# Expert layers with 64-column weight blocks on alternating column halves, tokens moving

## The chip, the cores and the metric

The kernel runs on one core of a Trainium2 chip. A core has a matrix engine (TensorE; PE for its matmuls and PEld for its weight loads in the trace), a vector engine (DVE), a scalar engine (ACT), GpSimd (POOL) and a queue engine (SP), which work beside each other and wait for each other by semaphores. Matmul results land in PSUM, eight banks of 512 fp32 values for each of 128 partitions; DVE and ACT read them there. A matmul has a stationary operand (`lhsT`, loaded into the array) and a moving one (`rhs`). The metric is device time of the whole kernel in microseconds, lower is better.

## What is computed

A recurrent attention block (rwkv7) makes 3072 tokens of 320 values each. Each token then goes to one of eight experts, at most 80 tokens for one expert:

```python
# x: (3072, 320), w1: (8, 320, 1024), w2: (8, 1024, 320), capacity 80
expert_idx = np.argmax(x @ w_gate, axis=1)
...
for e in range(E):
    tok_idx = np.where(expert_idx == e)[0]
    if len(tok_idx) > capacity:
        keep = np.argpartition(-gate_w[tok_idx], capacity)[:capacity]
        tok_idx = tok_idx[keep]
    h = np.maximum(x[tok_idx] @ w1[e], 0.0)
    out[tok_idx] = gate_w[tok_idx, None] * (h @ w2[e])
```

Everything is fp32.

## The kernel before

The attention stage takes most of the time. Its instructions are put in order by a planner in the kernel (class Plan); the change does not touch it. It works with 64x64 blocks on the four quarters of the matrix array, and it serves here as a place where small blocks can be seen: line 344 turns full 128x128 blocks (transposes by a matmul with the identity), and lines 437, 622, 655, 702 and 724 are each 16 matmuls on the four quarters.

Then the tokens of each expert are chosen (lines 1008 to 1051), which ends with the row numbers idx_g (to gather) and idx_s (to scatter). Meanwhile SP issues the weights of all experts, 2 x 320 x 1024 x 4 bytes = 2.6 MB for each, in four transfers: w1 (256 of the 320 input rows, line 978), w1r (the last 64 input rows; the first 512 hidden columns on partitions 0 to 63, the others on 64 to 127; line 980, two transfers) and w2 (line 981). Each expert has buffers of its own for them.

The expert stage is ordinary code on a tile framework, which sets the order of instructions and the semaphores by itself. For an expert e:

- gather (line 1063): POOL issues an indirect transfer of 80 token rows. All eight are issued first.
- turn_x (1067 to 1077): the rows are turned so that the 320 inputs lie on partitions (three transposes; the last 64 inputs twice, on both partition halves). DVE copies the result to xe.
- first_layer (1079 to 1091): xe is stationary (80 columns) and the weights move, 512 columns in each of four matmuls with all 128 rows (line 1085) and two with 64 rows, on the two row halves (line 1088). ACT applies relu into h, tokens on partitions.
- turn_h (1093 to 1101): eight transposes bring the 1024 hidden values onto partitions; DVE copies them to hT.
- second_layer (1103 to 1113): hT is stationary and w2 moves, eight matmuls of 320 columns into yp, tokens on partitions. DVE multiplies with the gate weight (line 1110) and POOL scatters the rows to the output (line 1111).

The main loop overlaps experts: the first layer of expert e, the turn of x for e+1, the second layer of e-1, the turn of h for e. An fp32 matmul stands in the trace as two records of TensorE (two passes), a transpose as one.

Of the kernel before, what the change touches and what calls it, by code (L numbers as in the profile page):

```python
# [8 lines left out]
F32 = mybir.dt.float32  # L9
# [3 lines left out]
Act = mybir.ActivationFunctionType  # L13
# [132 lines left out]
def kernel(  # L146
# [19 lines left out]
    nc = tc.nc  # L166
    B, H, S, D = r.shape
    N, DM = out.shape
    E = moe_w_gate.shape[1]
    F = moe_w1.shape[2]  # L170
# [885 lines left out]
    ps_h = ctx.enter_context(tc.tile_pool(name="ps_h", bufs=2, space=PSUM))  # L1056
    ps_t = ctx.enter_context(tc.tile_pool(name="ps_t", bufs=1, space=PSUM))
    ps_y = ctx.enter_context(tc.tile_pool(name="ps_y", bufs=1, space=PSUM))
    rows, xes, hs, hts = {}, {}, {}, {}

    def gather(e):
        rows[e] = fs.tile([cap, XW], F32, name="rows", tag="rows", bufs=8)
# [4 lines left out]
    def turn_x(e):  # L1067
        re = rows[e]
        tail = fs.tile([cap, 128], F32, name="twice", tag="twice")
        for i in range(2):  # L1070
            nc.scalar.copy(tail[:, 64 * i : 64 * i + 64], re[:, KW:DM])
        xp = ps_x.tile([128, 3, cap], F32, name="xp", tag="x")
        for i in range(2):
            nc.tensor.transpose(xp[:, i, :], re[:, 128 * i : 128 * i + 128], ident[:cap, :cap])
        nc.tensor.transpose(xp[:, 2, :], tail, ident[:cap, :cap])  # L1075
        xes[e] = fs.tile([128, 3, cap], F32, name="xe", tag="xe")
        nc.vector.tensor_copy(xes[e], xp)  # L1077

    def first_layer(e):
        w1, w1r, _ = weights[e]  # L1080
        xe = xes.pop(e)
        hp = [ps_h.tile([cap, FH], F32, name="hp", tag=f"h{j}") for j in range(2)]
        for i in range(2):
            for j in range(2):
                nc.tensor.matmul(hp[j], lhsT=xe[:, i, :], rhs=w1[:, i, FH * j : FH * j + FH], start=i == 0, stop=False)  # L1085
        for j in range(2):
            half = slice(64 * j, 64 * j + 64)
            nc.tensor.matmul(hp[j], lhsT=xe[half, 2, :], rhs=w1r[half, :], start=False, stop=True)  # L1088
        hs[e] = fs.tile([cap, F], F32, name="h", tag="h")
        for j in range(2):  # L1090
            nc.scalar.activation(hs[e][:, FH * j : FH * j + FH], hp[j], Act.Relu)  # L1091

    def turn_h(e):
        h = hs.pop(e)
        hts[e] = fs.tile([128, FK, cap], F32, name="hT", tag="hT")
        for j in range(2):
            tp = ps_t.tile([128, FK // 2, cap], F32, name="tp", tag=f"t{j}")
            for f in range(FK // 2):
                o = FH * j + 128 * f
                nc.tensor.transpose(tp[:, f, :], h[:, o : o + 128], ident[:cap, :cap])  # L1100
            nc.vector.tensor_copy(hts[e][:, FK // 2 * j : FK // 2 * (j + 1), :], tp)  # L1101

    def second_layer(e):
        w2 = weights[e][2]
        hT = hts.pop(e)
        yp = ps_y.tile([cap, DM], F32, name="yp", tag="y")
        for f in range(FK):
            nc.tensor.matmul(yp, lhsT=hT[:, f, :], rhs=w2[:, f, :], start=f == 0, stop=f == FK - 1)  # L1108
        y = fs.tile([cap, DM], F32, name="y", tag="y")
        nc.vector.tensor_scalar_mul(y, yp, rows[e][:, DM : DM + 1])  # L1110
        nc.gpsimd.indirect_dma_start(  # L1111
            out=out[:, :], out_offset=bass.IndirectOffsetOnAxis(ap=idx_s[:, e : e + 1], axis=0),
            in_=y[:, :], element_offset=0, bounds_check=N - 1, oob_is_err=False, in_offset=None)
# [4 lines left out]
    for e in range(E + 1):  # L1118
        if e < E:
            first_layer(e)  # L1120
        if e + 1 < E:
            turn_x(e + 1)
        if e > 0:
            second_layer(e - 1)
        if e < E:
            turn_h(e)


# [24 lines left out]
```

## Time and profile before

| what | value |
|---|---|
| median of 3 runs | 560.91 us (559.71 to 563.14) |
| the profiled execution's own time | 561.64 us |
| its span, first to last instruction | 559.6 us |
| TensorE busy with matmuls | 425.6 us, 76% of the span |
| DVE, ACT, POOL busy | 312.5, 186.0, 224.1 us |
| mean granted TensorE clock | 0.891 of 2.4 GHz |
| bytes moved by DMA | 72.91 MB, mean 130 GB/s |

The sums cover the whole span; the change concerns its last sixth alone, so they have to be read from that stretch. The slices of the page divide the span into 40 parts of 14 us, with the busy share of an engine in tenths; the timeline gives single groups of instructions in order of time, with start, length (from the first start to the last end) and count.

### The profile page before, as it was taken

Reading aid. Unit: us, or ns where it says so; the run is one execution under the profiler, and the core shown is the slowest. Engines: PE = TensorE matmul, PEld = TensorE weight load, DVE = VectorE, ACT = ScalarE, POOL = GpSimd, SP = SyncE. Lnnn points to the kernel's source line nnn. Section 1 sums busy time; section 2 is a strip of 40 time slices with the busy share of each in tenths; the row PEclk is TensorE's granted clock in tenths of the full one; section 3 lists DMA queues with packets and bytes.
Section 4 is the critical chain, followed back from the end, with each engine's and each line's share of the span. In section 5 each row is a group of like instructions: output and inputs, shape, how many; then the busy total and the mean of one; then the engine's idle time right before and its main releaser. Section 6 shows DMA issues by size and latency. Waiting matters only on the chain. (4 is left out here: it accounts for less than half of the span.)

```text
span 559.6 us, 22079 instructions
## 1 busy us (share of the span) xinstructions
PE 425.6 (76%) x9617; PEld 331.6 (59%) x9617; DVE 312.5 (56%) x706; ACT 186.0 (33%) x361; POOL 224.1 (40%) x393
## 2 busy tenths in 40 slices
PE   2644089797928988889799998998895003999996
PEld 2543078686717877778687887887784002344443
DVE  4867977444703855684476644966678981121211
ACT  2432064353512453444443643445231000101010
POOL 7010011788388410898699516981000005010101
PEclk9978569798976999999899999999699555899999
DMA  8775367556593477676577374327200049999300
GB/s 133 113 116 112 64 154 133 99 94 133 96 243 81 99 174 134 149 132 117 133 143 172 100 132 116 75 44 161 71 16 27 23 143 342 326 332 344 104 15 16
DMA packets 241444, 72.91 MB, mean 130 GB/s; under 512 B 217908, under 2 KB 235716, under 8 KB 241348
## 3 DMA queue, kind: packets, MB, share of 16 engines
q1 hardware_dynamic: 211428, 65.50, 51.6%
q10 hardware_dynamic: 29152, 4.36, 4.9%
q0 software_dynamic: 768, 1.64, 1.0%
q8 instruction: 76, 1.25, 0.9%
q14 instruction: 20, 0.16, 0.1%
HBM read 53.26 MB, written 18.13 MB: 128 GB/s over the span
## 5 line engine op out<-in xcount | busy, mean ns | idle before, releaser
L498 POOL TENSOR_TENSOR tmp<-lt 128x30 f32<-128x30 f32 (+9 forms) x150 | 84.0, 560 | 61.0 <-DMA lt<-blocks 50.3
L500 POOL TENSOR_TENSOR lt<-lt,tmp 128x30 f32<-128x30 f32 (+9 forms) x150 | 88.8, 592 | 11.8
L707 DVE TENSOR_TENSOR UL<-ps,mask 128x832 f32<-128x832 f32 x24 | 24.5, 1022 | 54.0 <-PE ps L702 54.0
L758 PE MATMUL ps<-wsel,xT 128*128 128x192 f32 x192 | 40.7, 360 | 2.3 <-DVE xT L748 1.4
L1111 POOL DMA_INDIRECT out_dram<-y,idx_s x8 | 7.3, 917 | 74.6 <-DVE y L1110 74.6
L758 PEld LDWEIGHTS ps<-wsel,xT 128*128 128x128 f32 x192 | 34.2, 208 | 4.3 <-DVE xT L748 1.7
L369 DVE TENSOR_TENSOR_SCAN P<-dec,begins 128x520 f32<-128x520 f32 x24 | 31.4, 1313 | 9.4 <-ACT dec L365 9.3
L1108 PE MATMUL yp<-w,hT 128*80 128x320 f32 x128 | 35.9, 434 | 0.5 <-DVE hT L1101 0.5
L344 PE MATMUL ps<-ident,raww 128*128 128x128 f32 x88 | 16.6, 320 | 25.5 <-DMA raww<-in_w_dram 24.4
L344 PE MATMUL ps<-ident,kb 128*128 128x128 f32 x192 | 32.8, 297 | 3.6 <-DVE ends L373 1.8
L735 DVE TENSOR_TENSOR st<-ps,st 128x832 f32<-128x832 f32 (+1 forms) x24 | 23.8, 990 | 17.9 <-PE ps L724 17.9
L485 POOL MEMSET nt<- 32x1024 f32 x12 | 11.3, 945 | 54.6 <-ACT nt L417 54.2
L377 DVE TENSOR_TENSOR_SCAN iv<-dec,ends 128x520 f32<-128x520 f32 x24 | 30.2, 1259 | 4.0 <-ACT ivc L396 3.3
L1085 PE MATMUL hp<-w,xe 128*80 128x512 f32 x64 | 31.6, 641 | 0.5 <-DVE xe L1077 0.5
L452 DVE TENSOR_TENSOR psi<-ps,mask 128x512 f32<-128x512 f32 x24 | 16.4, 686 | 27.3 <-PE ps L437 23.0
L1091 ACT ACTIVATE h<-hp 80x512 f32<-80x512 f32 x16 | 8.6, 587 | 61.5 <-PE hp L1088 61.5
L611 ACT COPY rv<-ps 128x1024 f32<-128x1024 f32 x24 | 24.3, 1014 | 11.4 <-PE ps L344 6.5
L344 PEld LDWEIGHTS ps<-ident,raww 128*128 128x128 f32 x88 | 11.5, 162 | 27.4 <-DMA raww<-in_w_dram 15.1
L1108 PEld LDWEIGHTS yp<-w,hT 128*80 128x80 f32 x128 | 18.6, 150 | 14.7 <-issue 0.8
L344 PEld LDWEIGHTS ps<-ident,kb 128*128 128x128 f32 x192 | 22.8, 149 | 7.4 <-issue 3.7
L407 DVE TENSOR_TENSOR kb<-rawkb,ps 128x640 f32<-128x640 f32 x22 | 17.9, 813 | 15.5 <-PE ps L344 13.4
L1077 DVE COPY xe<-xp 128x240 f32<-128x240 f32 x8 | 3.3, 407 | 40.9 <-PE xp L1075 40.9
(171 smaller groups left out, 961.3 us busy)
## 6 DMA issues: line engine op xcount, KB each, us to landing
w<-in_moe_w_dram SPq DMA_DIRECT2D x8, 1280.0 KB
w<-in_moe_w_dram SPq DMA_DIRECT2D x8, 1024.0 KB, 16.4
VL<-in_v_dram SPq DMA_DIRECT2D x96, 40.0 KB, 2.3
out_dram<-zero SPq DMA_DIRECT2D x8, 480.0 KB, 4.2
raww<-in_w_dram SPq DMA_DIRECT2D x44, 80.0 KB, 2.8
rawkb<-in_k_dram SPq DMA_DIRECT2D x44, 80.0 KB, 3.6
rawkb<-in_b_dram SPq DMA_DIRECT2D x44, 80.0 KB, 3.2
rawr<-in_r_dram ACTq DMA_DIRECT2D x84, 40.0 KB, 2.9
```

Of the source, the lines that this page charges most:

```text
L344: nc.tensor.matmul(o, lhsT=i, rhs=ident, start=True, stop=True, is_transpose=True, skip_group_check=True)
L369: nc.vector.tensor_tensor_scan(at("P", n), at("dec", n)[:, 0 : H * SEG], begins, 0.0, op0=Alu.mult, op1=Alu.add)
L377: nc.vector.tensor_tensor_scan(at("iv", n)[:, H * SEG : 0 : -1], at("dec", n)[:, H * SEG : 0 : -1], at("ends", n)[:, H * SEG : 0 : -1], 0. ...
L407: nc.vector.tensor_tensor(out=view(at("kb", n), 0, (HB * H, 2), (HB, H), (1, D)), in0=view(at("rawkb", n), 0, (DM, 2), (D, H), (1, D)), in ...
L498: e.tensor_tensor(out=tv, in0=t3[:, 0:s, s : s + 1].to_broadcast([128, s, n]), in1=t3[:, s : s + 1, s + 1 :].to_broadcast([128, s, n]), op ...
L500: e.tensor_tensor(out=t3[:, 0:s, s + 1 :], in0=t3[:, 0:s, s + 1 :], in1=tv, op=Alu.add)
L611: nc.scalar.copy(at("rv", n).rearrange("p (k c) -> p k c", k=2), ps[:, bank(kr) : bank(kr) + 2, :])
L707: nc.vector.tensor_tensor(out=view(at("UL", n), 0, (M4 * X, 2), (1, M4 * X)), in0=view(ps[:, bank(ku), :], 0, (512, 2), (1, M4 * X)), in1= ...
L735: nc.vector.tensor_tensor(out=view(st, o, (BS, M4), (step, 2), (1, n_)), in0=view(flat, 512 * bank(ky) + o, (4 * T, M4), (step, 2), (1, n_ ...
L758: nc.tensor.matmul(ps[:, b0, WS * m : WS * m + WX], lhsT=at("xT", n)[:, 2 * T * cof(m, 0) : 2 * T * cof(m, 0) + 2 * T], rhs=wsel_[:, WS * ...
L1085: nc.tensor.matmul(hp[j], lhsT=xe[:, i, :], rhs=w1[:, i, FH * j : FH * j + FH], start=i == 0, stop=False)
L1108: nc.tensor.matmul(yp, lhsT=hT[:, f, :], rhs=w2[:, f, :], start=f == 0, stop=f == FK - 1)
```

## The change

The expert layers swap their operands. In the first layer the weights are stationary, in blocks of 64 columns, and the 80 turned tokens move. Block b goes to column half 64 x (b mod 2) of the array, so that neighbours lie on different halves; the result has the hidden values on partitions, as the second layer needs them, and h is not turned any more. The 64 last input rows become 16 small matmuls on the four quarters. Relu is split: ACT takes the first half of the hidden values, DVE the second, both straight into hT.

In the second layer w2 is stationary in blocks of 64 of the 320 outputs, five for each of eight chunks of the hidden values, again on alternating column halves; the fifth block takes the one or the other half by turns, so that it is summed in two places. The result yp has the outputs on partitions and is copied to yT by DVE; turn_y turns it back with two transposes and one matmul against `pair`, two stacked 64x64 identities, which also adds the two halves of the fifth block. Then DVE scales as before and POOL scatters. `pair` is written by two copies on POOL. PSUM buffers: two of yp instead of one; one yq in place of two tp.

```diff
--- before.py
+++ after.py
@@ -1056,7 +1056,10 @@
     ps_h = ctx.enter_context(tc.tile_pool(name="ps_h", bufs=2, space=PSUM))
     ps_t = ctx.enter_context(tc.tile_pool(name="ps_t", bufs=1, space=PSUM))
     ps_y = ctx.enter_context(tc.tile_pool(name="ps_y", bufs=1, space=PSUM))
-    rows, xes, hs, hts = {}, {}, {}, {}
+    rows, xes, hts, yts = {}, {}, {}, {}
+    pair = fs.tile([128, HB], F32, name="pair", tag="pair", bufs=1)
+    nc.gpsimd.tensor_copy(pair[0:HB], ident[0:HB, 0:HB])
+    nc.gpsimd.tensor_copy(pair[HB:], ident[HB:, HB:])
 
     def gather(e):
         rows[e] = fs.tile([cap, XW], F32, name="rows", tag="rows", bufs=8)
@@ -1076,38 +1079,48 @@
         xes[e] = fs.tile([128, 3, cap], F32, name="xe", tag="xe")
         nc.vector.tensor_copy(xes[e], xp)
 
+    QF, NB = FK // 2, FH // 64
+
     def first_layer(e):
         w1, w1r, _ = weights[e]
         xe = xes.pop(e)
-        hp = [ps_h.tile([cap, FH], F32, name="hp", tag=f"h{j}") for j in range(2)]
+        hp = [ps_h.tile([128, QF, cap], F32, name="hp", tag=f"h{j}") for j in range(2)]
         for i in range(2):
             for j in range(2):
-                nc.tensor.matmul(hp[j], lhsT=xe[:, i, :], rhs=w1[:, i, FH * j : FH * j + FH], start=i == 0, stop=False)
-        for j in range(2):
-            half = slice(64 * j, 64 * j + 64)
-            nc.tensor.matmul(hp[j], lhsT=xe[half, 2, :], rhs=w1r[half, :], start=False, stop=True)
-        hs[e] = fs.tile([cap, F], F32, name="h", tag="h")
-        for j in range(2):
-            nc.scalar.activation(hs[e][:, FH * j : FH * j + FH], hp[j], Act.Relu)
-
-    def turn_h(e):
-        h = hs.pop(e)
+                for b in range(NB):
+                    c = 64 * (b % 2)
+                    nc.tensor.matmul(hp[j][c : c + 64, b // 2, :], lhsT=w1[:, i, FH * j + 64 * b : FH * j + 64 * b + 64],
+                                     rhs=xe[:, i, :], start=i == 0 and b < 2, stop=False, skip_group_check=True)
+        for b in range(NB):
+            c = 64 * (b % 2)
+            for j in range(2):
+                half = slice(64 * j, 64 * j + 64)
+                nc.tensor.matmul(hp[j][c : c + 64, b // 2, :], lhsT=w1r[half, 64 * b : 64 * b + 64],
+                                 rhs=xe[half, 2, :], start=False, stop=True, skip_group_check=True)
         hts[e] = fs.tile([128, FK, cap], F32, name="hT", tag="hT")
-        for j in range(2):
-            tp = ps_t.tile([128, FK // 2, cap], F32, name="tp", tag=f"t{j}")
-            for f in range(FK // 2):
-                o = FH * j + 128 * f
-                nc.tensor.transpose(tp[:, f, :], h[:, o : o + 128], ident[:cap, :cap])
-            nc.vector.tensor_copy(hts[e][:, FK // 2 * j : FK // 2 * (j + 1), :], tp)
+        nc.scalar.activation(hts[e][:, 0:QF, :], hp[0], Act.Relu)
+        nc.vector.tensor_scalar_max(hts[e][:, QF:, :], hp[1], 0.0)
 
     def second_layer(e):
         w2 = weights[e][2]
         hT = hts.pop(e)
-        yp = ps_y.tile([cap, DM], F32, name="yp", tag="y")
+        yp = ps_y.tile([128, 3, cap], F32, name="yp", tag="y", bufs=2)
         for f in range(FK):
-            nc.tensor.matmul(yp, lhsT=hT[:, f, :], rhs=w2[:, f, :], start=f == 0, stop=f == FK - 1)
+            for b in (0, 1, 2, 3, 4) if f % 2 == 0 else (1, 0, 3, 2, 4):
+                c = 64 * ((b + f) % 2) if b == 4 else 64 * (b % 2)
+                nc.tensor.matmul(yp[c : c + 64, b // 2, :], lhsT=w2[:, f, 64 * b : 64 * b + 64], rhs=hT[:, f, :],
+                                 start=f == 0 and b < 2, stop=f >= (FK - 2 if b == 4 else FK - 1), skip_group_check=True)
+        yts[e] = fs.tile([128, 3, cap], F32, name="yT", tag="yT")
+        nc.vector.tensor_copy(yts[e], yp)
+
+    def turn_y(e):
+        yT = yts.pop(e)
+        yq = ps_t.tile([cap, DM], F32, name="yq", tag="yq")
+        for i in range(2):
+            nc.tensor.transpose(yq[:, 128 * i : 128 * i + 128], yT[:, i, :], ident)
+        nc.tensor.matmul(yq[:, KW:], lhsT=yT[:, 2, :], rhs=pair, start=True, stop=True, skip_group_check=True)
         y = fs.tile([cap, DM], F32, name="y", tag="y")
-        nc.vector.tensor_scalar_mul(y, yp, rows[e][:, DM : DM + 1])
+        nc.vector.tensor_scalar_mul(y, yq, rows[e][:, DM : DM + 1])
         nc.gpsimd.indirect_dma_start(
             out=out[:, :], out_offset=bass.IndirectOffsetOnAxis(ap=idx_s[:, e : e + 1], axis=0),
             in_=y[:, :], element_offset=0, bounds_check=N - 1, oob_is_err=False, in_offset=None)
@@ -1120,10 +1133,11 @@
             first_layer(e)
         if e + 1 < E:
             turn_x(e + 1)
+        if e > 1:
+            turn_y(e - 2)
         if e > 0:
             second_layer(e - 1)
-        if e < E:
-            turn_h(e)
+    turn_y(E - 1)
 
 
 # ---- launch: one core; inputs and outputs as the reference has them ----
```

On TensorE the period of an expert is, before, this (expert 5's first layer to expert 6's; hp is the first layer's result, tp the turned h, yp the second layer's result; a row shows output, inputs, size and count):

```order
L1085 MATMUL hp<-w_5_7030,xe 80x512 x4
L1088 MATMUL hp<-w1r_7031,xe 80x512 x2
L1074 MATMUL xp<-ident,rows 128x80 x2
L1075 MATMUL xp<-ident,twice 128x80
L1108 MATMUL yp<-w_4_7025,hT 80x320 x8
L1100 MATMUL tp<-ident,h 128x80 x8
L1085 MATMUL hp<-w_6_7037,xe 80x512 x4
```

And in the changed kernel the same period is this (w_5_7030 and w1r_7031 are the first layer's weights of expert 5, w_4_7025 and w_5_7032 the second layer's of experts 4 and 5; yq is the turned y):

```order
L1092 MATMUL hp<-xe,w_5_7030 64x80 x32
L1098 MATMUL hp<-xe,w1r_7031 64x80 x16
L1111 MATMUL yp<-hT,w_4_7025 64x80 x28
L1077 MATMUL xp<-ident,rows 128x80 x2
L1078 MATMUL xp<-ident,twice 128x80
L1111 MATMUL yp<-hT,w_5_7032 64x80 x5
L1120 MATMUL yq<-ident,yT 80x128 x2
L1121 MATMUL yq<-pair,yT 80x64
L1111 MATMUL yp<-hT,w_5_7032 64x80 x17
L1092 MATMUL hp<-xe,w_6_7037 64x80 x32
```

22 matmuls and turns of an expert (besides those of x) have become 88 small matmuls and three turns, the second layer of an expert is cut into pieces around the next first layer, and turns of x and of y stand between its blocks.

The end on TensorE is, before, the second layers of experts 6 and 7 with the last turn of h between:

```order
L1088 MATMUL hp<-w1r_7045,xe 80x512 x2
L1108 MATMUL yp<-w_6_7039,hT 80x320 x8
L1100 MATMUL tp<-ident,h 128x80 x8
L1108 MATMUL yp<-w_7_7046,hT 80x320 x8
L1149 UNCONDITIONAL_BRANCH
```

In the changed kernel it is this:

```order
L1098 MATMUL hp<-xe,w1r_7045 64x80 x16
L1111 MATMUL yp<-hT,w_6_7039 64x80 x6
L1120 MATMUL yq<-ident,yT 80x128 x2
L1121 MATMUL yq<-pair,yT 80x64
L1111 MATMUL yp<-hT,w_7_7046 64x80 x40
L1120 MATMUL yq<-ident,yT 80x128 x2
L1121 MATMUL yq<-pair,yT 80x64
L1163 UNCONDITIONAL_BRANCH
```

The turn of y for expert 6 now stands ahead of the second layer of expert 7, and a turn of y follows the last matmul.

On POOL, the queue of the gathers in the changed kernel is this (iot_i and seg belong to the choice of tokens):

```order
L1003 IOTA iot_i 128x80
L1000 MEMSET seg 128x8
L1061 COPY pair<-ident 64x64
L1062 COPY pair<-ident 64x64
L1066 DMA rows<-x_rows,idx_g 80x321 x8
L1124 DMA out_dram<-y,idx_s 3072x320 x8
```

The two copies into pair are new and stand ahead of all gathers; the rest of POOL's order is as before.

## Rows read from the trace of the kernel before

**Rows 1.** The page's slices: TensorE busy and its clock in tenths, DMA in GB/s

```profile
PE   2644089797928988889799998998895003999996
PEclk9978569798976999999899999999699555899999
GB/s 133 113 116 112 64 154 133 99 94 133 96 243 81 99 174 134 149 132 117 133 143 172 100 132 116 75 44 161 71 16 27 23 143 342 326 332 344 104 15 16
```

**Rows 2.** Timeline, start and end of the experts: start us, length us, engine, line, operation

```profile
473.24 6.43 PE L1085 MATMUL hp<-w,xe 128*80 128x512 f32 x8 [0.50 <-DVE xe L1077]
...
550.37 4.54 PE L1108 MATMUL yp<-w,hT 128*80 128x320 f32 x16 [0.48 <-DVE hT L1101]
554.95 0.55 DVE L1110 TENSOR_SCALAR y<-yp,rows 80x320 f32<-80x320 f32 x1 [4.23 <-PE yp L1108]
```

**Rows 3.** Timeline of TensorE, expert 4's first layer to expert 5's

```profile
511.22 3.60 PE L1085 MATMUL hp<-w,xe 128*80 128x512 f32 x8
...
514.75 1.09 PE L1088 MATMUL hp<-w1r,xe 64*80 64x512 f32 x4
...
515.77 0.36 PE L1074 MATMUL xp<-ident,rows 80*128 80x80 f32 x2
...
515.97 0.23 PE L1075 MATMUL xp<-ident,twice 80*128 80x80 f32 x1
...
516.03 4.47 PE L1108 MATMUL yp<-w,hT 128*80 128x320 f32 x16
...
520.34 0.72 PE L1100 MATMUL tp<-ident,h 80*128 80x80 f32 x8
...
520.90 3.60 PE L1085 MATMUL hp<-w,xe 128*80 128x512 f32 x8
```

**Rows 4.** Timeline of TensorE in the attention stage, blocks on quarters and full turns

```profile
302.41 0.60 PE L344 MATMUL ps<-ident,VL 128*128 128x128 f32 x4
302.94 0.94 PE L702 MATMUL ps<-W,nt 64*64 64x104 f32 x32
303.71 0.89 PE L724 MATMUL ps<-VL,kb 64*64 64x104 f32 x32
304.53 0.66 PE L344 MATMUL ps<-ident,rawa 128*128 128x128 f32 x4
...
306.47 0.90 PE L724 MATMUL ps<-UL,kb 64*64 64x104 f32 x32
307.19 0.64 PE L622 MATMUL ps<-rv 64*64 64x64 f32 x32
```

**Rows 5.** Groups from 434 us on: DVE's PSUM copies, busy us, mean ns | idle

```profile
L1101 DVE COPY hT<-tp 128x320 f32<-128x320 f32 x16 | 7.1, 478 | 0.4 <-PE tp L1100 0.4
...
L1077 DVE COPY xe<-xp 128x240 f32<-128x240 f32 x8 | 3.3, 407 | 40.9 <-PE xp L1075 40.9
```

**Rows 6.** Groups of the whole run: POOL's small copies

```profile
L809 POOL COPY xg<-gsm 128x4 f32<-128x4 f32 x5 | 1.2, 246 | 17.3 <-DVE gsm L806 17.3
L306 POOL COPY gt<-ident 32x256 f32<-32x256 f32 x2 | 0.8, 392 | 0.1
```

**Rows 7.** Timeline of POOL: the first gather and what ended the idle time before

```profile
465.16 1.13 POOL L1063 DMA_INDIRECT rows<-x_rows,idx_g  x1 [10.09 <-DVE idx_s L1051]
```

**Rows 8.** Stretches: length, PE, PEld, DVE, ACT, POOL busy, PEclk, DMA share, GB/s

```profile
470.00:480.00 10.00, 7.56 (x13) 2.58 (x15) 0.41 (x1) 1.17 (x6) 3.62 (x4) 0.56 1.06 311
480.00:490.00 10.00, 9.68 (x42) 4.17 (x39) 1.79 (x4) 2.71 (x8) 0.00 (x0) 1.00 1.07 350
...
522.00:524.00 2.00, 2.00 (x6) 0.60 (x4) 0.00 (x0) 0.00 (x0) 0.28 (x1) 1.00 0.30 91
524.00:526.00 2.00, 2.00 (x11) 0.65 (x10) 0.09 (x1) 0.39 (x1) 0.00 (x0) 1.00 0.00 0
```

**Rows 9.** Line 980, transfers of w1r: duration, first and last start, time to landing

```profile
L980 SPq DMA_DIRECT2D w1r<-in_moe_w_dram x16: 477/596/1194, 454.5 to 508.5; - x16
...
DMA to landing us min/median/max: 5.7/12.5/15.0
```

## The prediction

> **What bounds the kernel now.** I read the page's slices first. The last eight of 40, some 112 us, hold the choice of tokens and then the experts; TensorE's slices there read 9 from 476 us to 546 us, and the rate of the DMA falls from over 320 GB/s to nothing while TensorE goes on [rows 1]. Then the timeline of that stretch. The first matmul of expert 0 starts at 473.24 and the last of expert 7 ends at 550.37 + 4.54 = 554.91 [rows 2]: **81.67 us of experts**, followed by one scaling on DVE and one scatter. Then one expert in the middle, expert 4 to expert 5: from 511.22 to 520.90 is a period of **9.68 us** in which TensorE is never free [rows 3]. So the engine that the change rewrites is the bound. The windows say what stands behind it: the clock is at its half level (1.2 GHz) until about 478.8 and then at 2.4 GHz, and the weights stream at about 300 GB/s and more until about 523 us, when expert 5 of 8 is computed [rows 8]. The weights are well ahead, but only by about two and a half experts.
>
> **What the period is made of.** An fp32 matmul stands in the trace as two records, two passes. The sixteen passes of 320 columns take 516.03 to 520.34 = 4.31, 0.269 us each, so a pass of 512 columns takes 0.43 and the eight of the first layer 3.44; the four 64-row passes run two and two, 0.86; the turns of x take 0.20 to 0.26; the eight turns of h from 520.34 to 520.90 = 0.56, so 0.070 us for 80 moving columns [rows 3].
>
> **The price of a new step.** After the change a pass moves 80 columns against 64 stationary ones, and neighbours lie on different column halves. No row of before has full rows with half columns. The nearest is the attention stage: 64x64 blocks on all four quarters of the array, where 32 passes of 104 columns take 306.47 to 307.19 = 0.72 us [rows 4]. One after another they would take 32 x 0.09 = 2.9, so four run at once, two of each four on the same rows and different column halves. A step there is 0.72/8 = 0.090 us for 104 columns and (0.64 - 0.23)/7 = 0.059 for 64 (eight steps last 0.64 to the end of the last one [rows 4]; a single short pass lasts 0.23 [rows 3]); at 80 columns in proportion **0.071**, and the turns of h, a full array with 80 columns, give 0.070 [rows 3]. I take 0.071 for a step in which both halves work. The bounds: 0.067 below, by columns from the pass of 320 (80/320 of 0.269), 0.142 above, if the halves do not work together.
>
> **The sum for one expert.** The first layer has 32 matmuls of full rows, 16 pairs in two passes = 32 steps, and 16 matmuls on quarters, 4 fours in two passes = 8 steps. The second has 40 matmuls = 40 steps. 80 steps x 0.071 = 5.68. Turning x stays, 0.20 [rows 3]. The turns of h go. Turning y back is new: two turns with 128 moving columns, 0.108 each (the four from 302.41 to 302.94 less a joint of 0.10), and one small matmul in two passes of 64 columns, 2 x 0.059 [rows 4]: 0.33. Together **6.21 us** in place of about 9.3 of bare work.
>
> **Joints.** Where the shape of the blocks changes (full, column halves, quarters) the trace shows a gap: 514.75 stands 0.09 after the eight passes of 0.43 from 511.22, 515.77 stands 0.16 after its two times 0.43 [rows 3], 302.94 and 304.53 some 0.10 after theirs [rows 4]. The period before has two or three; the order of the changed kernel has 38 from the first expert to the last matmul of expert 7, since turns of x and y are put between the blocks of the second layer. I take 0.12 each, **4.6 us**; bounds 0 (if full rows with half columns need no change) and 0.16, 6.1.
>
> **The whole stretch.** 8 x 6.21 = 49.7, less the first turn of x, which lies ahead of 473.24, and the last turn of y, which is in the tail: 49.1. The first layer of expert 0 runs at 1.2 GHz as it does now (6.43 for what takes 3.60 later [rows 2, 3]): 40 steps more, +2.8. Waits that nothing covers: the second layer of expert 0 needs hT through PSUM, a DVE pass of 0.48 [rows 5] beside the turn of x, 0.3 left; at the end the turn of y of expert 6 needs its copy yT (0.41 as the copy xe of the same shape [rows 5], and 0.1 of signals), while DVE still has hT of expert 7, and the second layer of expert 7 queues behind that turn: 0.55; elsewhere five passes of the next expert and a turn of x cover it, 0.35 in all for what they don't. 1.2. Sum 49.1 + 2.8 + 4.6 + 1.2 = **57.7 us against 81.67: 24.0 saved.**
>
> **What is given back.** POOL gets two copies of 64x64 into pair, and all eight gathers are queued behind them; the first gather starts at 465.16, as soon as DVE releases it [rows 7], so the copies lie on the path. Bounds by POOL's small copies, 0.25 to 0.39 each [rows 6]: 0.5 to 0.8, I take **0.5**. In the tail the scaling of y waited for the last pass alone; now a copy of 0.41 [rows 5], two signals, a joint and the turn of 0.33 come between: **1.1**. Relu goes from two ACT passes to one on ACT and one on DVE beside each other; each engine has under 2 us of work in 6.8 us of expert, so it costs nothing but the wait counted above. The attention stage keeps its instructions and order.
>
> 24.0 - 0.5 - 1.1 = 22.4. The profiled execution took 561.64, so 539.2; it stands 0.7 above the median of the runs shown, 560.91. **I predict 538.5 us.**
>
> **Do the weights follow?** The period becomes 6.21 + about 0.6 = 6.8 us, and an expert's 2.6 MB of weights at some 330 GB/s [rows 1] take 7.9, so TensorE gains a microsecond on the stream with each expert. Counted back from 473.7 + 57.7 = 531.4, the first layer of expert 7 starts about 524. The last transfer of w1r is issued at 508.5 and lands 12.5 us later by the median, 521 [rows 9]; the stream ends by 524 [rows 8]. That holds with 1 to 3 us to spare. If the steps or joints are cheaper, the stream becomes the bound: 521 + 7.5 for what follows is 528.5, that is 2.9 earlier, so nothing much under 535.5 is to be had.
>
> [...] In the trace the eight turns of h load 128 stationary columns each on the same 80 rows, and the passes still start every 0.070 us [rows 3]: the loads hide behind the passes. [...]
>
> **Rivals.** (1) *The halves do not work together.* Every matmul of full rows then stands alone: 8 x 36 pairs x 2 x 0.071 = 40.9 us more, 579, slower than before. For it: more columns are moved (88 x 80 against 6 x 512 + 8 x 320 + 8 x 80, the fp32 passes alike), and no row shows full rows on half columns. Against it: the quarters share rows and work together [rows 4]. It turns from gain to loss at a step of 0.071 + 22.4/576 = 0.110 us. Chance 0.06. (2) *The loads do not hide.* An exposed load of 128 columns costs about 0.06: the two turns from 515.77 to 515.97 take 0.20 and not 0.14 [rows 3]. So 0.03 for 64 columns, on 576 steps +17, 556; with the loads of both halves one after another +35, 573. Chance 0.05. (3) *The joints eat more.* 0.25 a joint (+5), a wait of 0.5 at each turn of y (+3), or one more layer at 1.2 GHz (+2.8): 546 to 553, still faster. Chance 0.10. (4) *Less overhead, and the weights are the bound*: about 535.5, chance 0.10, inside the range.
>
> **How the numbers follow.** The forecast with rival 4 holds 0.78, 534 to 546; the rest is 0.01. The range 534 to 548 adds a part of rival 3 and leaves out about 0.18. One per cent, 5.6 us, is about what a measurement of this kernel can tell from no change: faster by more 0.88 (forecast, 3 and 4), within it 0.04, slower by more 0.08 (rival 1 and part of 2).
>
> **What would show it.** Passes of both layers that start in pairs a few ns apart, a new pair every 0.07 us; 6.5 to 7 us from one expert's first layer to the next one's; gaps of 0.1 at the changes of shape; the last scaling of y at about 532.6 in place of 554.95 [rows 2]; the clock at 2.4 GHz from about 479 to the end; the first gather 0.5 later. Pairs that start 0.14 apart mean rival 1, 0.10 to 0.13 rival 2. TensorE waiting for w1r or w2 of the last experts would mean rival 4. I am wrong if the first two layers of one expert together take over 8 us at 2.4 GHz.

## The result and the profile after

The changed kernel took 555.51 us in the median of 20 runs (548.42 to 561.58), the kernel before 560.86 (20 runs, 555.05 to 570.76). The ratio is **0.9887, 95% interval 0.9861 to 0.9914**: faster by 1.1%, some 5 to 6 us, where 22.4 us (to 538.5) was forecast. The ratios in this text are taken from the runs in the chip's faster state alone, and are not those of the medians. The direction was right, the size was not, and the time lies above the range. The profiled execution took 556.64 us (span 554.9).

The page's slices of the kernel after, rows as in [rows 1], with the load row PEld left out:

```profile
PE   2754199797929988989898998999888102788795
...
PEclk9978569989866998988899799999699755688799
...
GB/s 135 116 114 113 65 171 145 90 116 123 122 214 61 118 170 132 148 138 121 127 139 188 50 150 124 84 31 121 117 26 28 2 24 335 324 333 330 289 15 20
```

The slices of the experts (the 35th and on, from about 472 us) show what went wrong before any detail does: TensorE reads 7, 8, 8, 7 and then 9, its clock 6, 8, 8, 7 and then 9, where [rows 1] has 9 throughout and a clock of 8 and then 9. Both are low while the DMA moves some 290 to 330 GB/s, and recover once it stops.

The timeline of TensorE in the kernel after (start us, length us, engine, line, operation, count of passes, and in brackets the idle time before and what ended it). L1092 is the first layer, L1098 its remainder on quarters, L1111 the second layer, L1120 and L1121 the turn of y:

```profile
475.78 4.53 PE L1092 MATMUL hp<-xe,w 128*64 128x80 f32 x64 [0.50 <-DVE xe L1080]
480.25 1.27 PE L1098 MATMUL hp<-xe,w1r 64*64 64x80 f32 x32
...
482.66 2.39 PE L1092 MATMUL hp<-xe,w 128*64 128x80 f32 x63
484.98 0.78 PE L1098 MATMUL hp<-xe,w1r 64*64 64x80 f32 x32
...
488.39 0.93 PE L1092 MATMUL hp<-xe,w 128*64 128x80 f32 x21
491.57 3.19 PE L1092 MATMUL hp<-xe,w 128*64 128x80 f32 x42 [2.25 <-issue]
...
498.26 1.39 PE L1111 MATMUL yp<-hT,w 128*64 128x80 f32 x33 [0.16 <-issue]
...
504.67 0.35 PE L1098 MATMUL hp<-xe,w1r 64*64 64x80 f32 x3 [2.04 <-issue]
...
514.76 2.01 PE L1111 MATMUL yp<-hT,w 128*64 128x80 f32 x51
519.62 1.60 PE L1111 MATMUL yp<-hT,w 128*64 128x80 f32 x19 [2.85 <-issue]
...
545.07 3.00 PE L1111 MATMUL yp<-hT,w 128*64 128x80 f32 x80
```

The experts now last from 475.78 to 545.07 + 3.00 = 548.07: **72.29 us**, against 81.67 before and 57.7 forecast. Three readings. First, the steps are as forecast: 80 passes in 3.00 are 40 steps, (3.00 - 0.23)/39 = 0.071 us each, and 63 passes in 2.39 give 0.070. Second, there are pauses in the middle of a layer, in a row of passes that need nothing new: 2.25, 0.16, 2.04 and 2.85, together **7.3 us**, put down to "issue", that is, the engine waited for nothing that the profile shows. The kernel before had none. Third, after the three long pauses the same work takes up to twice its time: 42 passes take 3.19 where 63 took 2.39.

The stretches of that (length, busy time of PE and passes, granted clock, share of the DMA engines, GB/s):

```profile
491.57:494.69 3.12, 3.12 (x42) 0.50 1.04 397
505.20:508.60 3.40, 3.40 (x45) 0.50 1.09 315
508.60:510.10 1.50, 1.50 (x46) 0.99 1.06 397
518.90:525.60 6.70, 5.98 (x66) 0.50 1.01 283
```

At the granted clock of 0.50 TensorE is busy for 3.12 + 3.40 + 5.98 = 12.5 us, and half of that, **6.25 us**, would not be there at 1.00, where a pass takes 2.39/63 = 0.038 us and not 3.12/42 = 0.074. 72.29 less 7.3 less 6.25 is 58.7, within 1.0 of the 57.7 forecast. So nearly the whole miss of this stretch is in the pauses and the clock.

What are the pauses? The rows from 491.57 to the pause before 498.26 hold 127 passes, those from there to the pause before 504.67 again 127, and those from there to the pause before 519.62 hold 254. Each pass has a load, and with the few instructions that only set or await a semaphore the trace has 255 or 256 instructions of TensorE in the first two stretches and 512 in the third. The page names a DMA queue for instructions, q8; its rows (packets, MB, share of the DMA engines) in the kernel before and after:

```profile
q8 instruction: 76, 1.25, 0.9%
```

```profile
q8 instruction: 85, 1.39, 1.0%
```

The rows of the stretch from 470 to 525 us, after first (q1 carries the weights):

```profile
q1 hardware_dynamic: 9542, 16.63, 98.6%
...
q8 instruction: 7, 0.11, 0.9%
```

```profile
q1 hardware_dynamic: 9154, 16.12, 93.9%
...
q8 instruction: 2, 0.03, 0.2%
```

Over the whole run there are nine packets more than the 76 of before, for 10,769 matmuls and as many loads in place of 9,617 and as many: 2,304 instructions in 9 packets, **256 instructions in a packet of 16.4 KB**. All of TensorE's matmuls and loads by 256 give 84.1 packets after and 75.1 before, so the 85 and 76 carry TensorE's instructions. The pauses stand at the seams between packets. During the weights' stream TensorE needs 7 of them in place of 2, from DMA engines that the weights keep busy for 98.6% of the time.

The trace's record of DMA packets ties the two together. Each packet of q8 has its own times there (the DMA view of a short window, such as 488.9 to 490.1 us, shows it alone in q8). One ends at 490.07, in the first pause, and TensorE goes on at 491.57. The next packets end at 496.91, 503.25, 510.50 and 518.16; TensorE goes on after its pauses at 498.26, 504.67 and 519.62, that is 1.35 to 1.50 us after a packet each time. (The packet of 510.50 met a TensorE that had run at a granted clock of 0.50 until 508.6 and was not yet through its instructions: no pause.)

The tail, rows of the timeline of all engines in the kernel after:

```profile
548.11 0.41 DVE L1114 COPY yT<-yp 128x240 f32<-128x240 f32 x1 [2.39 <-PE yp L1111]
...
549.16 0.55 DVE L1123 TENSOR_SCALAR y<-yq,rows 80x320 f32<-80x320 f32 x1 [0.64 <-PE yq L1121]
550.70 0.92 POOL L1124 DMA_INDIRECT out_dram<-y,idx_s  x1 [3.78 <-DVE y L1123]
```

And the last scatter of the kernel before:

```profile
555.77 0.91 POOL L1111 DMA_INDIRECT out_dram<-y,idx_s  x1 [4.67 <-DVE y L1110]
```

From the last pass (548.07) to the scaling of y are 1.09 us, where the kernel before had 0.04: 1.1 more was forecast. But the scatter starts 0.99 after y is done (549.71), where the kernel before took 0.27 (y done at 554.95 + 0.55 [rows 2], scatter at 555.77). The scatter before it was issued only 4.7 us earlier, against 5.6 in the kernel before, and by the DMA packets its rows had ended only at 549.45, 1.25 us before the late one starts. The same 1.25 us (1.24 in e4) stands in e1, e4, e5 and e7, whose last scatters are late too, while in the kernel before the rows had ended 3.55 us earlier. So the late scatter is read as waiting for the one before it, though the view names DVE; no run tried it.

### The profile page after: what moved, and what is told of

Same layout as the page of the kernel before. It is cut to its first block, busy times and chain, and to the rows that moved or that the text cites. A ratio compares the mean times of both kernels' runs of the same rounds, so it can differ in the third digit from the quotient of the medians.

```text
span 554.9 us, 24379 instructions
## 1 busy us (share of the span) xinstructions
PE 418.9 (75%) x10769; PEld 363.9 (66%) x10769; DVE 311.2 (56%) x706; ACT 182.0 (33%) x353; POOL 224.7 (40%) x395
## 5 line engine op out<-in xcount | busy, mean ns | idle before, releaser
L498 POOL TENSOR_TENSOR tmp<-lt 128x30 f32<-128x30 f32 (+9 forms) x150 | 86.1, 574 | 60.5 <-DMA lt<-blocks 49.7
L758 PE MATMUL ps<-wsel,xT 128*128 128x192 f32 x192 | 38.4, 344 | 2.3 <-DVE xT L748 1.4
L758 PEld LDWEIGHTS ps<-wsel,xT 128*128 128x128 f32 x192 | 31.8, 196 | 4.4 <-DVE xT L748 1.7
L1111 PE MATMUL yp<-hT,w 128*64 128x80 f32 x640 | 29.6, 249 | 3.2 <-issue 3.0
L452 DVE TENSOR_TENSOR psi<-ps,mask 128x512 f32<-128x512 f32 x24 | 16.4, 688 | 25.4 <-PE ps L437 23.5
L1111 PEld LDWEIGHTS yp<-hT,w 128*64 128x64 f32 x640 | 26.6, 148 | 5.0 <-issue 3.5
L655 PE MATMUL ps<-VL,psi 64*64 64x104 f32 x768 | 27.2, 289 | 0.5 <-DVE VL L628 0.3
L1092 PE MATMUL hp<-xe,w 128*64 128x80 f32 x512 | 24.3, 259 | 2.8 <-issue 2.3
L1092 PEld LDWEIGHTS hp<-xe,w 128*64 128x64 f32 x512 | 23.1, 159 | 3.3 <-issue 2.4
```

The lines of the kernel that those rows point to most:

```text
L498: e.tensor_tensor(out=tv, in0=t3[:, 0:s, s : s + 1].to_broadcast([128, s, n]), in1=t3[:, s : s + 1, s + 1 :].to_broadcast([128, s, n]), op ...
L655: nc.tensor.matmul(ps[T * x : T * x + T, b0 + q, X * i : X * i + X], lhsT=psi[rows, q, i, :], rhs=at("VL", n)[rows, vo : vo + X], start=i ...
L758: nc.tensor.matmul(ps[:, b0, WS * m : WS * m + WX], lhsT=at("xT", n)[:, 2 * T * cof(m, 0) : 2 * T * cof(m, 0) + 2 * T], rhs=wsel_[:, WS * ...
L1092: nc.tensor.matmul(hp[j][c : c + 64, b // 2, :], lhsT=w1[:, i, FH * j + 64 * b : FH * j + 64 * b + 64], rhs=xe[:, i, :], start=i == 0 and ...
L1111: nc.tensor.matmul(yp[c : c + 64, b // 2, :], lhsT=w2[:, f, 64 * b : 64 * b + 64], rhs=hT[:, f, :], start=f == 0 and b < 2, stop=f >= (FK ...
```

## The experiments

Theory A: TensorE runs out of instructions, because their blocks come by DMA engines that are full of weights; the clock falls after these pauses. Rivals: the pauses belong to the sequence itself (a buffer, a semaphore), or to long transfers that a block has to sit out; or the steps depend on something else than the two column halves.

**e1 and e2: no weights beside the experts.** The weights of expert 0 are loaded last, so that the experts start when nearly everything has landed, in the changed kernel (e1) and in the kernel before (e2):

```
-    for e in range(E):
+    for e in [*range(1, E), 0]:
         load_expert(e)
```

> The changed kernel with the weights of expert 0 issued last, so that no expert can start before the stream of weights is nearly over; the instructions of TensorE are the same. Theory A: the three pauses of 2 to 3 us are TensorE waiting for its own instructions, whose transfers stand behind the weights on the DMA engines. Then the pauses are gone, the clock stays at 2.4 GHz after the first layer, and from the first matmul of expert 0 to the last of expert 7 it takes 56 to 60 us (72.3 less 7.3 of pauses and 6.8 of half clock). Theory B: the small blocks run dry by themselves (TensorE's queue, semaphores, buffers), whatever the DMA does: the pauses stay and the stretch is 68 to 73 us. The whole time grows under both, to about 587 or 600, since the experts start some 45 us later.

> The kernel before with the same delay of expert 0's weights, as a control. Theory A says that it never ran out of instructions, since its large matmuls need five times fewer: the stretch from the first matmul of expert 0 to the last of expert 7 stays at 81.7 us, within 1. If a busy DMA slows TensorE in some other way (operand reads, semaphores), it becomes shorter, by 2 us or more. Whole time about 610.

Measured: 579.56 us and 604.34, one run each. TensorE's timeline of e1:

```profile
516.90 4.53 PE L1092 MATMUL hp<-xe,w 128*64 128x80 f32 x64 [42.44 <-DMA w<-in_moe_w_dram]
...
528.22 2.38 PE L1092 MATMUL hp<-xe,w 128*64 128x80 f32 x64
...
534.77 2.38 PE L1092 MATMUL hp<-xe,w 128*64 128x80 f32 x64
...
568.48 2.56 PE L1111 MATMUL yp<-hT,w 128*64 128x80 f32 x66
```

No pause put down to issue is left, and from 516.90 to 571.04 the experts take 54.1 us, 18 less than in the changed kernel and under the 56 to 60 that was expected; the period is 6.55 us from one first layer to the next. The framework put the work in a somewhat different order here (second layers in one piece, fewer joints), so not all of the 18 is the pauses' and the clock's. In e2 the period stays at 9.68:

```profile
534.55 3.60 PE L1085 MATMUL hp<-w,xe 128*80 128x512 f32 x8
...
544.23 3.60 PE L1085 MATMUL hp<-w,xe 128*80 128x512 f32 x8
```

Its stretch is 517.51 to 597.59 = 80.1 us, 1.6 less than the 81.67 of before. That lies between the two expectations (within 1, or 2 and more). 1.2 of it is the first layer of expert 0, 5.26 in place of 6.43: the granted clock rose to 1.00 at 478.87 in the kernel before, 5.63 us after the start of the experts, and in e2 at about 3.3 after it, an estimate: its 5.26 is 1.66, half of 3.3, over the 3.60 of a later first layer. A period in the middle gains nothing from an empty DMA. With no stream beside them the experts of the two kernels differ by 80.1 - 54.1 = 26.0 us, more than the 24.0 forecast.

**e3: half the instructions.** The first layer in the new form, the second as before: w2 moving against hT, no turn of y and no pair.

```
+        yp = ps_y.tile([cap, DM], F32, name="yp", tag="y")
         for f in range(FK):
-            for b in (0, 1, 2, 3, 4) if f % 2 == 0 else (1, 0, 3, 2, 4):
-                ...
+            nc.tensor.matmul(yp, lhsT=hT[:, f, :], rhs=w2[:, f, :], start=f == 0, stop=f == FK - 1)
...
-        if e > 1:
-            turn_y(e - 2)
```

> The first layer of the changed kernel with the second layer of before: hT is stationary, w2 moves 320 columns, y comes out with tokens on partitions, no turn of y, no pair. An expert needs 115 passes instead of 187, in a longer time. Theory A: instructions are then used up more slowly than they arrive under the weights (one block of them in 6.5 to 7.5 us), no pause over 0.5 us, clock at 2.4 GHz; by the steps 2.84 + 0.20 + 4.31 + 0.36 = 7.7 us an expert, 65 us for the stretch, 544 us in all, 0.97 of before. Theory B, pauses by the small blocks: some of them remain in the first layer, 549 to 553.

Measured: **544.06 us** (542.79 to 549.35), ratio 0.9661 (0.9588 to 0.9734), beside 0.9887 for the whole change. An expert has 183 passes in the changed kernel, not the 187 of the expectation. Of the pauses two small ones are left, where none over 0.5 was expected: early, where two first layers follow each other closely, and 127 passes apart, a packet; and one before the last second layer, which has to wait for its single PSUM buffer until the y before it is scaled:

```profile
485.57 0.65 PE L1095 MATMUL hp<-xe,w1r 64*64 64x80 f32 x24 [0.84 <-issue]
...
493.67 0.49 PE L1095 MATMUL hp<-xe,w1r 64*64 64x80 f32 x10 [0.39 <-issue]
...
538.07 4.50 PE L1106 MATMUL yp<-w,hT 128*80 128x320 f32 x16 [0.69 <-issue]
```

The first two end 1.35 and 1.45 us after a packet of instructions; the nearest packet before the last one ended 9 us earlier, and e6 takes it away with a second buffer. The "issue" of the last row is therefore another thing than that of the first two, though it has the same name. The experts take 476.08 to 542.57, 66.5 us. More arithmetic time than the whole change, fewer instructions, and 11 us faster.

**e4: shorter transfers.** The changed kernel with w1 in two transfers and w2 in four.

```
-        nc.sync.dma_start(w1, moe_w1[e, 0:KW, :].rearrange("(c p) f -> p c f", p=128))
+        for c in range(2):
+            nc.sync.dma_start(w1[:, c], moe_w1[e, 128 * c : 128 * c + 128, :])
...
-        nc.sync.dma_start(w2, moe_w2[e].rearrange("(c p) d -> p c d", p=128))
+        for c in range(0, FK, 2):
+            nc.sync.dma_start(w2[:, c : c + 2], moe_w2[e, 128 * c : 128 * c + 256, :].rearrange("(c p) d -> p c d", p=128))
```

> The changed kernel with the transfers of weights cut: w1 in two, w2 in four, same bytes and same sizes of descriptors. Theory A in the form that an instruction transfer waits until the part of a weight transfer that a DMA engine is at is through: the parts are half and a quarter as long, the pauses shrink from 2 to 3 us each to under 1, the clock drops go with them, 541 to 548 us. If the instruction transfers wait for something else (the sheer load of the DMA engines, or memory), the pauses stay and the time is that of the changed kernel, 553 to 556. Theory B expects the same 553 to 556.

Measured: 554.67 us, ratio 0.9832 (0.9748 to 0.9915), not told apart from the changed kernel. The pauses stay: 1.73 and 1.34, then 2.04 and 3.05 at the places of the changed kernel's last two, and 1.21 more at 528 (one of 0.21 in the very first layer is at no packet); two of them:

```profile
499.19 1.39 PE L1113 MATMUL yp<-hT,w 128*64 128x80 f32 x33 [1.34 <-issue]
...
520.27 1.47 PE L1113 MATMUL yp<-hT,w 128*64 128x80 f32 x18 [3.05 <-issue]
```

The five each end 1.3 to 1.5 us after a packet of instructions. So the length of a weight transfer as it is issued does not decide how long a packet waits. That it is the load of the full engines instead is what is left; this run does not show it.

**e5: four blocks of a half, then four of the other.** The order of the blocks alone is changed.

```
-                for b in range(NB):
+                for b in [*range(0, NB, 2), *range(1, NB, 2)]:
...
-            for b in (0, 1, 2, 3, 4) if f % 2 == 0 else (1, 0, 3, 2, 4):
+            for b in (0, 2, 4, 1, 3) if f % 2 == 0 else (0, 2, 1, 3, 4):
```

> The changed kernel with one thing different: the blocks no longer alternate between the column halves; all even blocks come first, then all odd ones. Theory A (it is the alternation that lets two passes run at once; the pauses of the changed kernel are TensorE waiting for instructions while the weights load): passes of the same half follow each other singly, each about 2 x 0.069 = 0.139 us, so 72 matmul pairs cost about 10.0 us and an expert about 11.4 us; instructions are then used up more slowly, some 30% slower than the blocks arrive, so that pauses nearly vanish; stretch of the experts 92 to 95 us, total 575 to 582 us. Rival (passes run together by queueing ahead, whatever half they stand on): step stays at 0.069 us, pauses as in the changed kernel, total about 555 us.

Measured: 559.48 us in one run. Neither expectation held: the first layer takes 3.05 in place of 2.38 and the second about 3.2 in place of 3.0, not 4.4 and 5.5:

```profile
520.74 0.98 PE L1111 MATMUL yp<-hT,w 128*64 128x80 f32 x19 [2.10 <-issue]
...
533.91 3.05 PE L1092 MATMUL hp<-xe,w 128*64 128x80 f32 x64
...
542.23 3.05 PE L1092 MATMUL hp<-xe,w 128*64 128x80 f32 x64
```

Runs of four blocks are eight passes, 0.56 us if each stands alone. Sixteen passes, eight on each half, take 3.05/4 = 0.76: between 0.56 (all in pairs) and 1.11 (none). So a pass whose half is free seems to start ahead of those that wait for the other half, but only from a few places behind. The timeline bears this out at a joint: from 490.33 to 490.49 three passes of a first layer and the last three of a second layer start by turns, one by one, although the two passes of a matmul belong together. Its pauses (1.54, 1.38, 1.34, 0.45, 2.10, 0.93) are 7.7 us in sum, a little more than the changed kernel's. They stand 126 to 128 passes apart, 255 or 256 instructions each time, so here one stands at every packet. The clock does not fall after them: after the longest, from 520.7 to 522.0, the granted clock is 1.00.

**e9: long runs on one half**, to settle that. All blocks of a layer on the lower half, then all on the upper:

```
-        for i in range(2):
-            for j in range(2):
-                for b in range(NB):
+        for s, i, j in [(s, i, j) for s in range(2) for i in range(2) for j in range(2)]:
+                for b in range(s, NB, 2):
...
-        for f in range(FK):
-            for b in (0, 1, 2, 3, 4) if f % 2 == 0 else (1, 0, 3, 2, 4):
-                c = 64 * ((b + f) % 2) if b == 4 else 64 * (b % 2)
+        for s, f in [(s, f) for s in range(2) for f in range(FK)]:
+            for b in (s, s + 2, 4) if f % 2 == s else (s, s + 2):
+                c = 64 * s
```

> The changed kernel with long runs on one column half: of each layer all blocks of the lower half first (32 passes of the first layer, 16 of the remainder, 40 of the second), then all of the upper half. Theory L (TensorE starts a waiting pass ahead of its turn when its own half is free, but reaches only some three passes ahead, as the kernel with short runs of 8 and 12 showed): within a run the passes follow each other singly, 0.069 us each; first layer about 64 x 0.069 = 4.3 us against 2.38, second about 80 x 0.069 = 5.4 against 2.99, remainder 1.1 against 0.78; period about 11.5 us; instructions are used up at less than half the rate, so pauses vanish; total 575 to 582 us. Rival P (passes run two at a time whatever half they stand on): first layer still 2.4 to 3.1 us, total 555 to 560 us.

Measured: 578.27 us in one run, with full steps of one pass:

```profile
483.68 4.37 PE L1091 MATMUL hp<-xe,w 128*64 128x80 f32 x64
487.99 1.11 PE L1097 MATMUL hp<-xe,w1r 64*64 64x80 f32 x32
...
511.21 5.53 PE L1110 MATMUL yp<-hT,w 128*64 128x80 f32 x80
...
555.58 4.37 PE L1091 MATMUL hp<-xe,w 128*64 128x80 f32 x64
```

64 x 0.069 = 4.4 and 80 x 0.069 = 5.5: theory L holds. (The kernel before took 564.70 beside this run.) The DMA view from 470 to 525 us, and the window from 483 to 570:

```profile
q1 hardware_dynamic: 9358, 16.39, 99.1%
```

```profile
483.00:570.00 87.00, 86.25 (x1355) 1.00 0.54 163
```

So this kernel, with the instructions of the changed one in number and form and the same stream of weights, has **no pause for issue and the full clock** from 483 to 570 us. Its period is (555.58 - 483.68)/6 = 12.0 us. Counted on in steps of 256 instructions, its packets under the stream end 2.5 to 4.9 us before TensorE needs them, where the pauses show 1.2 to 1.5 as the least. It uses its instructions slowly enough.

**e7: half the weights.** Experts 4 to 7 use the tiles of experts 0 to 3, so that only half is loaded.

```
-    for e in range(E):
+    for e in range(E // 2):
         load_expert(e)
+    for e in range(E // 2, E):
+        weights[e] = weights[e - E // 2]
```

> The changed kernel, but experts 4 to 7 use the weights of experts 0 to 3, so only half of the weights are loaded (left out: the loading and the use of the own weights of experts 4 to 7); instructions of TensorE are the same in number and form. Theory A (TensorE waits for its instructions, whose blocks share the DMA engines with the weights): the weights' stream ends at about 488 us, pauses and the half clock that follows them stop there; the first pause at most remains, 543 to 546 us. Rival (the pauses belong to this instruction sequence itself, or to a wait of TensorE on something other than DMA traffic): pauses at the same places, 555 us.

Measured: 540.72 us (536.97 to 541.91), ratio 0.9623 (0.9571 to 0.9674). In the timeline one pause is left; it ends at 487.51, as the weights' stream ends (the slices of the DMA read 9 until 487.4 and fall then), and none follows although the instructions are the same in number and form (their order differs, as in e1):

```profile
487.51 3.19 PE L1094 MATMUL hp<-xe,w 128*64 128x80 f32 x42 [2.47 <-issue]
...
528.66 2.57 PE L1113 MATMUL yp<-hT,w 128*64 128x80 f32 x66
```

In windows of the same run, after that pause and from then on:

```profile
487.50:490.60 3.10, 3.09 (x42) 0.50 0.29 92
491.40:530.00 38.60, 38.60 (x1063) 1.00 0.07 20
```

TensorE is busy for all of 38.60 us, at the full clock. The experts take 471.44 to 531.23 = 59.8; less the pause and the half clock (2.47 + 1.55) that is 55.8. Theory A had said 543 to 546: it was too cautious by 2 to 5 us. The rival, pauses at the same places and 555, is out: the one pause that is left ends 1.53 us after a packet of instructions.

**e6: two buffers for y in the hybrid of e3.**

```
-        yp = ps_y.tile([cap, DM], F32, name="yp", tag="y")
+        yp = ps_y.tile([cap, DM], F32, name="yp", tag="y", bufs=2)
```

> The hybrid (first layer in the new form, second layer as before) with two PSUM buffers for y instead of one. The hybrid's last second layer stood idle 0.69 us until the y before it had been scaled. If that wait is on the path: 0.7 us less than the hybrid, about 543.3 us. Rival (something else is late next, the h of the same expert): within 0.2 us of 544.0.

Measured: 545.5 us (543.06 to 550.1), ratio 0.9729 (0.9679 to 0.9778), not told apart from e3. In the trace the pause of 0.69 is gone (the last two second layers follow each other without a gap), and one early pause of 0.23 is left. What 0.7 us is worth cannot be read from runs that lie 7 us apart: inconclusive.

**e8: the new second layer only where no weights stream.** The hybrid, with the second layers of experts 5 and 6 in blocks.

```
+    BLOCKS = (5, 6)
...
+            (second_layer if e - 1 in BLOCKS else second_rows)(e - 1)
```

> The hybrid, but with the second layer in the new form for experts 5 and 6 alone, which come after most of the weights have landed, so that the extra instructions do not have to share the DMA engines with them. Theory A: no new pauses; each of the two second layers saves about 1 us, total 541.5 to 542.5 us against the hybrid's 544. Rival (the turning back of y and its joints eat the gain, or the pauses come anyway): 544 to 546 us.

Measured: 543.29 us (538.14 to 548.5), ratio 0.9658 (0.9609 to 0.9707): faster than both kernels, and not told apart from e3. In the trace no pause for issue is left, not even the two early ones of e3, and a second layer in blocks takes 2.99 in place of 4.47:

```profile
505.98 2.43 PE L1093 MATMUL hp<-xe,w 128*64 128x80 f32 x64
...
513.72 2.43 PE L1093 MATMUL hp<-xe,w 128*64 128x80 f32 x64
...
517.16 2.99 PE L1112 MATMUL yp<-hT,w 128*64 128x80 f32 x80
519.98 2.38 PE L1093 MATMUL hp<-xe,w 128*64 128x80 f32 x64
```

The period that holds it is 6.26 us (513.72 to 519.98) after 7.74. That agrees with the expectation for the layers; whether the whole run gains the 2 us is not settled by these runs.

## Why the prediction was wrong

**The failed step** is in the sum of the whole stretch: "Waits that nothing covers ... 1.2", with the clock "at 2.4 GHz from about 479 to the end". The waits were looked for among data and engines. That TensorE has to be fed with instructions too was no term, and 7.3 us of pauses stand in place of none. The granted clock, which stood at 0.50 with each of the three long pauses, for 3.1 to 6.7 us, cost another 6.25. None of the four rivals has this, nor does the sign under which the forecast called itself wrong (two layers over 8 us: they take 6.15 in e1). The measured 555.51 stands beside the 556 of rival 2 by chance, since the steps are 0.071. Rival 3 had "one more layer at 1.2 GHz (+2.8)" among its mishaps, but not what would cause it, and less than half of the price. The traces give the clock as a share of the full one: where the forecast has 1.2 and 2.4 GHz, they show 0.50 and 1.00.

**The same oversight in "Do the weights follow?"** The weights did follow: no pass waits for one. The question asked what TensorE wants from the stream, and not what else wants the same engines. That the question was open could be read in the profile of before: its queue of instructions with 76 packets, its counts of matmuls and loads, and DMA engines that are full until about 522 us [rows 8]. How long a packet takes beside the weights could not, as the kernel before never waited for one. With the packets of 256 instructions:

- before: 8 + 4 + 3 + 16 + 8 = 39 passes in a period of 9.68 us [rows 3], 78 instructions: a packet per 32 us; no pause
- e9: 64 + 32 + 3 + 4 + 80 = 183 passes in 12.0 us: a packet per 8.4, under the stream one per 7.2 to 9.5; no pause
- e3: 64 + 32 + 3 + 16 = 115 passes in 7.75 us: a packet per 8.6; two small pauses near the start, where the order is denser, 8.1 us from one to the next
- e5: 183 passes in 8.3 us (533.91 to 542.23): a packet per 5.8 wanted; pauses 6.3 to 7.5 us apart
- the change: 183 passes in 6.55 us (e1): a packet per 4.6 wanted; pauses, and from pause to pause two packets in 13.1 (491.57 to 504.67) and 14.95 us, that is 6.6 and 7.5 a packet

So with full DMA engines a packet came every 6.3 to 8.1 us to a TensorE that stood waiting (the longest in e3, 8.0 in e4), and the kernels that want one less often ran free (e9) or nearly so (e3). When the weights are gone or not there (e1, e7, and this kernel after about 526), one per 4.6 us was no trouble. That the weights' stream causes the pauses and that the rate of instructions decides is shown by e1, e7 and e9 together: the first two take the stream away, the third keeps it and uses the instructions more slowly. That it is the instructions' packets which come late is shown by the packets themselves: all 19 pauses for issue that stand at a seam between packets, in six kernels (this one and e3 to e7), end 1.2 to 1.5 us after a packet of q8 has ended. The packet itself is not slow: in the changed kernel it moves in 1.1 to 1.3 us beside the weights and in 0.9 to 1.4 once they have landed. It is late to start: counted on from the pauses in steps of 256 instructions, it starts 3.4 to 5.0 us after TensorE has begun on the packet before it, and 0.1 to 0.6 us after that once the weights have landed. Why it starts so late beside a full queue of weights stays open; e4 excludes the length of a weight transfer.

**Step by step**, the rest of the forecast:

- *The price of a new step*, 0.071: measured 0.071 and 0.070. The bound of 0.142 for halves that do not work together is twice e9's 0.069 a pass.
- *The first layer of expert 0 at the low clock*, nearly as forecast: 475.78 to 481.52 = 5.74 (granted clock 0.51 from 475.78 to 481.40) where 482.66 to 485.76 = 3.10 is the time at 1.00, 2.6 more (forecast 2.8).
- *The sum for one expert and the joints*, 6.21 + about 0.6 = 6.8: 6.55 in e1. A joint there is 0.09 (first layer to its remainder), forecast 0.12.
- *What is given back*: the two copies for pair run while POOL would have waited anyway: the first gather starts 3.89 us after the matmul ids_p (467.96 - 464.07), before 3.80 (465.16 - 461.36). From the matmul ids_p to the first matmul of the experts are 475.78 - 464.07 = 11.71 us after and 473.24 - 461.36 = 11.88 before; forecast 0.5 more, measured none. The scaling of y starts 1.05 later after the last pass than before (forecast 1.1), but the late scatter adds 0.7.
- *Rival 2*, loads that do not hide: its chance of 0.05 was right. 80 passes, whose blocks are all on the same 128 rows, start in pairs every 0.071 us, so the loads are hidden.
- *Rival 1*, halves that do not work together: did not come about in this kernel; e9, whose blocks do stand alone, took 578.27, next to the 579 of this rival.

The account of the profiled execution, 556.64 against the 539.2 forecast for one: pauses +7.3, clock +6.25, the rest of the stretch +1.0; the tail from the last pass to the end of the span 6.83 in place of 4.69 + 1.1, +1.0; the start of the experts 475.78 in place of 473.74, +2.0, which lies before the changed code (the matmul ids_p ran 2.7 later, and starts anywhere from 457.05 in e8 to 466.11 in e6) and is the spread of single runs; outside the span -0.3. Sum 17.3 of 17.4.

## What to carry to other kernels

Count instructions as a transfer: where small blocks multiply the matmuls and loads, divide the instructions of a period by those in a packet of the instruction queue (256 here), and compare with how often a packet can arrive while the DMA engines are full (every 6.3 to 8.1 us here). If it is wanted more often, use the small blocks only where the stream has ended or where they save most per instruction; here the first layer alone in blocks (e3) won 3.4% where both layers won 1.1%. A pause that the profile puts down to "issue" in the midst of passes with nothing new to wait for is read by counting the instructions from one to the next, and by the time at which the last packet of the instruction queue ended.

## What the runs showed that was not expected

- TensorE seems to start a pass ahead of its turn when its column half is free, from a few places behind: runs of eight passes on one half cost 0.76 us for sixteen, not 1.11 (e5), while runs of 32 and 40 pay the full 0.069 a pass (e9).
- With pauses of 2.04 to 2.85 us the granted clock was at 0.50 for 3.1 to 6.7 us in the changed kernel, and with 2.47 in e7; after 2.10 in e5 it stayed at 1.00. Where no such pause stood it did not fall: in e9 it was 1.00 from 483 to 570, and in e1 every first layer from expert 1 on took 2.38 to 2.43 us, its time at 1.00. So in the experts a pause goes with each fall, but its length alone does not decide; what does stays open.
- The quarters (64 x 64 blocks) take 0.78 us for 32 passes, and 1.11 when the column halves come one after the other (e9).
